# Weight casts, sums and norm scales at other places in the queues of a three-stage fp32 kernel

## The chip, the cores and the metric

The kernel runs on one core of one Trainium2 chip. The metric is the device time of one execution in microseconds, the median of three runs. The engines are called by the short names that the profile uses: PE (TensorE's matmuls; PEld are its weight loads), ACT (ScalarE), DVE (VectorE), POOL (GpSimd) and SP (SyncE, which here issues all DMAs). Each engine works through its own queue in the order in which the program was written.

## The reference

Three stages follow each other, all in fp32: attention with a window, an MLP, and a gated MLP behind an RMS norm. The change touches the end of the second stage and the third.

```
x = attention(q, k, v)                    # 4 x 576 tokens, d = 512, window 128
h = x @ w_in                              # first MLP: 512 -> 2048 -> 512
x = (h * clip(h + 3, 0, 6) / 6) @ w_out
xn = x / sqrt(mean(x * x) + 1e-6) * rms_g # second MLP: 512 -> 2 x 1536 -> 512
g = xn @ w_gate
out = (g * sigmoid(g) * (xn @ w_val)) @ w_out2
```

## The kernel before

**Precision.** Matmuls run on fp32r operands. Each fp32 operand is split into a high part (a cast, made by ACT) and a low part (the rest, a subtraction on DVE), and each product is three matmuls: high x high, high x low, low x high. So every weight and every activation needs one cast and one subtraction before PE can use it.

**First MLP.** The 2304 tokens are taken in six blocks of 384. A block has 16 steps `m`, each with 12 matmuls into the one bank `ps_h` (L465), an activation of two operations (ACT's Relu L693, DVE's `t` L694, which reads `ps_h` and so frees it), the split of the result (ACT `g` L699, DVE `g` L705), and nine matmuls of the second product of the step before (L478).

**Second MLP.** The tokens are taken in three superblocks `s` of 768, and the 1536 hidden columns in 12 chunks `m`. One pair of superblock and chunk is a group `i = 12 s + m`, so there are 36. A group is a 2x2 block product made with seven products instead of eight (`group`): the right operands are seven sums or parts of the inputs (A11, S2, A12, S3, S1, A22, S4), the left ones seven sums or parts of a chunk's weights (B11, T2, B21, T3, T1, T4, B22). Each product is six matmuls of 384 columns (L797) into one of three banks. In a group, ACT copies the first product (`s`, L810), DVE adds it twice (`u`, L813 behind product 1 and L820 behind product 3), and so on; product 2 waits for the copy `s`, product 3 for the first `u`, product 6 for the first `t` (L824), since they add into the banks that these read. The last operation is `t·r` (L834); its cast and subtraction (`g`, L840 and L842) are made within the next group. After the groups m = 0, 2, 4, 6, 8 and 11 comes a round of outputs (`outputs`): six tiles of six matmuls of 512 columns (L853), each added by DVE to `y` (L860), or copied by ACT (L858) in the first round of a superblock. The banks of even and odd groups alternate.

**Weights of the second MLP.** A chunk is read from DRAM as four parts (`load`, tile `tx`, into one of two stages). POOL makes four sums from them (`sums`, L239 to L242), ACT casts them in two halves of 1024 and 768 columns (`high`, L248, tile `th`; the first half needs the third sum), and DVE subtracts in the same halves (`low`, L256, tile `tl`). Both are stored to DRAM as well, and superblocks 1 and 2 fetch them from there (L766) into a ring of three places. Superblock 0 uses what was just made: chunks 0, 1, 2, 11, 10 and 9 are prepared in the last block of the first MLP (EARLY), chunks 3 to 8 in the groups 1 to 6 (the rest of `parts`). Of EARLY the j-th loads at step 2j + 1, sums at 2j + 2, casts at 2j + 3 and 2j + 4, and subtracts at 2j + 4 and 2j + 5.

**Inputs.** The first MLP's result is normed (`Norm`: squares on ACT, the root on POOL, the scale on DVE, L515, then transposes on PE, a copy `yt` on ACT, L520, and a store). A superblock's inputs are loaded as `x2raw` (`Inputs`), scaled by `rms_g` in four parts (L619), added to S1, S2, S4 and S3, and split (L643 on ACT, L647 on DVE). For superblocks 1 and 2 this is done during the superblock before: load after its group 5, scale on DVE after group 7, sums on POOL after group 8, the splits of A11 and S2 after groups 9 and 10, and the other five in group 11 and its outputs, each as soon as PE has used the old one.

Of the kernel before, what the change touches and what calls it, by code (L numbers as in the profile page):

```python
# [10 lines left out]
F32 = mybir.dt.float32  # L11
# [4 lines left out]
AF = mybir.ActivationFunctionType  # L16
ALU = mybir.AluOpType
# [3 lines left out]
P = 128  # L21
B, H, S, D = 4, 8, 576, 64
# [3 lines left out]
KC = DM // P  # L26
F1, F2 = 2048, 1536
M1, M2 = F1 // P, F2 // P
# [41 lines left out]
def fused_kernel(ctx: ExitStack, tc: tile.TileContext, qd, kd, v, w1, w2, rms_g, out):  # L70
# [199 lines left out]
    class Pair:  # L270
# [335 lines left out]
    class Inputs:  # L606
# [2 lines left out]

        def __init__(self, s):  # L610
            self.s, self.n = s, 3 * P
            self.x = xpool.tile([P, KC, 6 * P], F32, tag="xs", name="x2raw")
            sp.dma_start(out=self.x, in_=x2[s])

        def block(self, r, c):
            return self.x[:, 2 * c : 2 * c + 2, r * self.n : (r + 1) * self.n]

        def scale(self, c):
            vec.tensor_scalar(self.x[:, c], self.x[:, c], g_sb[:, c : c + 1], None, ALU.mult)  # L619

        def sum(self, which, on, out):
            setattr(self, which, out)
            x, sub = self.block, on.tensor_sub
            if which == "S1":
                on.tensor_add(out, x(1, 0), x(1, 1))
            elif which == "S2":
                sub(out, self.S1, x(0, 0))
            elif which == "S3":
                sub(out, x(0, 0), x(1, 0))
            else:  # L630
                sub(out, x(0, 1), self.S2)

        def of(self, which):
            return getattr(self, which) if which[0] == "S" else self.block(int(which[1]) - 1, int(which[2]) - 1)
# [13 lines left out]

    ops = {}

    early = [Parts(m, STAGES[j % 2], (RING + SCRATCH)[j]) for j, m in enumerate(EARLY)]
    parts = {m: Parts(m, STAGES[m % 2 == 0], RING[m % 3]) for m in range(3, M2 - 3)}
    outs, slot, late = None, AHEAD, []
    for p, (b, m0, m1) in enumerate(PARTS):
        n = BLOCKS[b][1]
# [13 lines left out]
        for m in range(m0, m1):  # L669
# [58 lines left out]
            if last:  # L728
                if m == 1:
                    fed = Inputs(0)  # L730
                elif m == 2:
# [46 lines left out]
                x.pop(which)()  # L778
        waiting[:] = [x for x in waiting if x]

    def group(i, after):


        s, m = divmod(i, M2)
# [5 lines left out]
        new = parts.get(i + 2)  # L790
        odd = m % 2

        def product(k, ps, start=True):
            x, w, j = ops[s, k], ring[i] if i in ring else parts[i].tiles(), 0
            for c in range(2):
                for a, b in PARTS_OF:
                    pe.matmul(  # L797
                        ps, lhsT=w[a][:, k, c * P : (c + 1) * P], rhs=x[:, b, c],
                        start=(start and j == 0), stop=(j == 5), skip_group_check=True,
                    )  # L800
                    j += 1
            after(k)

        if new and odd:
            new.high(0)
            new.low(0)
        product(0, ps_1)
        if i and i + 3 in parts:
            parts[i + 3].load()
        act.copy(s1, ps_1)  # L810
        settle("high")
        product(1, ps_6)
# [1 line left out]
        settle("low")  # L814
        product(2, ps_1, False)
        act.activation(r[:, 0], ps_1, AF.Silu)
        if new:
            new.high(odd)
        product(3, ps_6, False)
        vec.tensor_add(u[:, 1], s1, ps_6)  # L820
        if new and odd:
            new.low(1)
# [5 lines left out]
        if new and not odd:  # L828
            new.high(1)
        if i + 3 in parts:  # L830
            parts[i + 3].sums()
        product(6, ps_5, False)
        vec.tensor_add(t[:, 0], u[:, 0], ps_5)
        vec.tensor_mul(t, t, r)  # L834
        if i + 3 not in ring and i + 3 not in parts:
            fetch(i + 3)

# [3 lines left out]

        waiting.append({"high": high, "low": lambda: vec.tensor_sub(gs[i][:, 1], t, f32(gs[i][:, 0]))})  # L842

    def outputs(i, spare, after=lambda t: None):


        s, m = divmod(i, M2)
        for t in range(6):
            p, tag = ((ps_out, "o2"), (ps_a, "T"), spare)[t % 3]
# [14 lines left out]
            after(t)  # L864
        fetch_out(i + 4)

    for i in range(M2 * PAIRS2):
        s, m = divmod(i, M2)
        for x in norms:
            x.store()  # L870
            x.scale()
        turn = m == M2 - 1 and s + 1 < PAIRS2
        group(i, (lambda k: fed.high(k) if k > 1 else None) if turn else lambda k: None)
        if i == 0:
            finish1()
            fetch_out(0)
            fetch_out(2)
        if s + 1 < PAIRS2:
            if m == 5:
                fed = Inputs(s + 1)  # L880
            elif m == 7:
                for c in range(KC):
                    fed.scale(c)
            elif m == 8:
                sums = xpool.tile([P, 4, 2, n], F32, tag="xs", name="sums")
                for k in range(4):
                    fed.sum(f"S{(1, 2, 4, 3)[k]}", pool, sums[:, k])
            elif m in (9, 10):
                fed.high(m - 9)
                fed.low(m - 9)  # L890
        spare = banks[(i + 1) % 2][2]
        if m == 0 and s or m in (2, 4, 6, 8):
            x = parts.get(i + 2)
            outputs(i - 2, spare, lambda t: x.low(t // 2) if x and t in (0, 2) else None)
        elif m == M2 - 1:
            outputs(i - 3, spare, lambda t: fed.low(t + 1) if turn and 0 < t else None)
            if turn:
                fed.low(2 + 4)
        if i:
            norms[:] = [x for x in norms if x.back()]  # L900
    settle("high")
    settle("low")
    outputs(M2 * PAIRS2 - 2, banks[0][2])
    p2.close()


# [41 lines left out]
```

## Time and profile before

| | |
|---|---|
| median of 3 runs | 988.22 us (987.93 to 988.41) |
| the profiled execution | 987.71 us; its span, first to last instruction, 985.7 us |
| mean granted clock of PE | 0.996 |
| busy PE / DVE / ACT / POOL | 961.9 / 631.8 / 463.6 / 164.1 us |
| first MLP's last block to its end | until 553.65 us |
| second MLP, superblocks 0 / 1 / 2 from | 553.65 / 693.26 / 834.17 us |

All times in rows are microseconds from the start of the span. The busy times are means over all stages. The engine with the most is PE, and in the timelines an idle stretch of an engine is written in brackets behind the instruction that ended it, with what released it.

### The profile page before, as it was taken

The page shows a single profiled execution, that of the slowest core. Times are in us where ns is not written, and L with a number is a line of the kernel's source. Part 1 is how long each engine was busy: PE and PEld are TensorE (multiplying, and loading weights), DVE is VectorE, ACT ScalarE, POOL GpSimd, SP SyncE. Part 2 cuts the span into 40 slices and gives each one's busy share as a digit, 9 for nine tenths or more (in the row PEclk, how much of TensorE's full clock was granted, in tenths as well). Part 3 has the DMA queues.
Part 4 walks back from the last instruction along what each step waited for, and adds up shares of the span by engine and source line. Part 5 has one row for each costly group of instructions (what it writes and reads, how often), then busy time and mean ns, then how long its engine had stood idle before and what let it go on. Part 6 is the DMA issues. An engine that isn't in the chain of part 4 may idle for free.

```text
span 985.7 us, 14697 instructions
## 1 busy us (share of the span) xinstructions
PE 961.9 (98%) x5448; PEld 845.4 (86%) x5448; DVE 631.8 (64%) x1297; ACT 463.6 (47%) x961; POOL 164.1 (17%) x257
## 2 busy tenths in 40 slices
PE   8999899999999999999998999999999999999998
PEld 5677788888888888888997888989899988999996
DVE  6788863445777766765576657777645678545654
ACT  6799854455666665665454453314132214132120
POOL 4333111121112211111043333130000030000000
PEclk9999999999999999999999999999999999999999
DMA  6446401113665465445356756956655756655521
GB/s 238 150 164 226 180 30 31 49 41 94 190 202 189 151 183 174 154 141 159 128 187 241 286 197 247 335 222 233 232 202 195 275 183 244 241 218 192 202 108 65
DMA packets 67719, 176.85 MB, mean 179 GB/s; under 512 B 5056, under 2 KB 41920, under 8 KB 62912
## 3 DMA queue, kind: packets, MB, share of 16 engines
q1 hardware_dynamic: 67648, 175.92, 50.9%
q8 instruction: 43, 0.70, 0.3%
q14 instruction: 28, 0.23, 0.1%
HBM read 131.86 MB, written 44.04 MB: 178 GB/s over the span
## 4 chain that ended last, share of the span: by engine, by line
PE 83%; DVE 8%; ACT 4%; issue 2%; DMA 1%; POOL 1%; SPq 0%; POOLq 0%; ACTq 0%; DVEq 0%
PE ps_h L465 17%; PE ps_o L478 17%; PE ps_y L853 14%; PE ps_o L797 9%; PE ps_S L797 7%; PE ps_A L797 5%; PE ps_h L797 3%; PE ps_av L402 3%; PE ps_t L389 3%; PE ps_s L349 1%; PE ps_s L340 1%; ACT wx L132 1%; PE warm L553 1%; DVE t L694 1%; DVE y L860 1%
## 5 line engine op out<-in xcount | busy, mean ns | idle before, releaser
L465 PE MATMUL ps_h<-xs,w 128*128 128x384 f32 x1152 | 225.1, 344 | 3.1 <-DVE t L694 3.1
L478 PE MATMUL ps_o<-w,g 128*128 128x512 f32 x864 | 223.7, 401 | 3.0 <-DVE w L143 2.6
L465 PEld LDWEIGHTS ps_h<-xs,w 128*128 128x128 f32 x1152 | 203.8, 191 | 8.8 <-DVE t L694 4.4
L478 PEld LDWEIGHTS ps_o<-w,g 128*128 128x128 f32 x864 | 157.1, 188 | 43.0 <-issue 6.1
L853 PE MATMUL ps_y<-wo,g 128*128 128x512 f32 x648 | 150.7, 390 | 0.5 <-DVE g L842 0.5
L853 PEld LDWEIGHTS ps_y<-wo,g 128*128 128x128 f32 x648 | 121.2, 188 | 25.7 <-DVE g L842 0.9
L694 DVE SCALAR_TENSOR_TENSOR t<-t,ps_h 128x384 f32<-128x384 f32 x96 | 53.2, 554 | 138.6 <-ACT t L693 138.6
L693 ACT ACTIVATE t<-ps_h,three 128x384 f32<-128x384 f32 x96 | 55.7, 580 | 102.2 <-PE ps_h L465 92.8
L377 POOL TENSOR_SCALAR r<-den 128x2 f32<-128x2 f32 x72 | 30.4, 423 | 347.0 <-ACT t L375 345.6
L860 DVE TENSOR_TENSOR y<-y,ps_y 128x512 f32<-128x512 f32 x90 | 61.4, 685 | 37.0 <-PE ps_y L853 36.8
L375 ACT ACTIVATE t<-t,m 128x256 f32<-128x256 f32 (+1 forms) x144 | 69.4, 485 | 7.9 <-DVE m L363 7.9
L699 ACT CAST g<-t 128x384 fp32r<-128x384 f32 x96 | 49.5, 516 | 49.0 <-DVE t L694 45.9
L827 ACT ACTIVATE r<-r 128x384 f32<-128x384 f32 x36 | 18.9, 526 | 113.2 <-DVE r L826 113.2
L797 PE MATMUL ps_o<-S,tw 128*128 128x384 f32 x336 | 65.9, 338 | 0.0
L705 DVE TENSOR_TENSOR g<-t,g 128x384 fp32r<-128x384 f32 x96 | 54.8, 571 | 13.0 <-ACT g L699 11.6
L797 PEld LDWEIGHTS ps_o<-S,tw 128*128 128x128 f32 x336 | 59.4, 188 | 0.4 <-DVE u L813 0.4
L378 POOL TENSOR_TENSOR r<-r,minus 128x2 f32<-128x2 f32 x72 | 56.4, 784 | 6.0
L810 ACT COPY s<-ps_S 128x384 f32<-128x384 f32 x18 | 8.6, 480 | 94.6 <-PE ps_S L797 94.6
L389 PE MATMUL ps_t<-ident,t 128*128 128x128 f32 x272 | 42.2, 275 | 5.2 <-DVE t L383 4.3
L363 DVE CUSTOM_DVE_ANT_0 t<-ps_s,rel 128x256 f32<-128x256 f32 (+2 forms) x128 | 44.7, 394 | 3.3 <-PE ps_s L349 3.3
L394 ACT COPY pt<-ps_t 128x512 f32<-128x512 f32 (+1 forms) x72 | 40.0, 555 | 13.1 <-PE ps_t L389 12.9
L389 PEld LDWEIGHTS ps_t<-ident,t 128*128 128x128 f32 x272 | 33.0, 140 | 14.7 <-ACT t L375 4.3
(135 smaller groups left out, 1472.7 us busy)
## 6 DMA issues: line engine op xcount, KB each, us to landing
tw<-t SPq DMA_DIRECT2D x54, 896.0 KB, 6.3
wraw<-w SPq DMA_DIRECT2D x36, 512.0 KB, 4.3
wo<-w SPq DMA_DIRECT2D x18, 1024.0 KB, 4.8
wraw<-w SPq DMA_DIRECT2D x16, 1024.0 KB, 7.6
t<-th SPq DMA_DIRECT2D x12, 896.0 KB, 4.0
t<-tl SPq DMA_DIRECT2D x12, 896.0 KB, 4.2
b<-wx SPq DMA_DIRECT2D x24, 256.0 KB, 2.5
w<-w SPq DMA_DIRECT2D x12, 512.0 KB, 2.8
```

The costliest lines, as they stand in the source:

```text
L375: act.activation(p, p, AF.Exp, bias=self.m[:, a : a + 1], scale=-1.0, accum_out=self.den[:, a : a + 1])
L378: pool.tensor_tensor(self.r, self.r, minus, ALU.pow)
L389: pe.transpose(self.ps[:, a, c], self.t[:, a, c * P : (c + 1) * P], ident)
L465: pe.matmul(ps[:, : n * P], lhsT=w[:, a, c * P : (c + 1) * P], rhs=xs[c][:, b, : n * P], start=(k == 0), stop=(k == 3 * KC - 1),)
L478: pe.matmul(o, lhsT=g[:, a, i * P : (i + 1) * P], rhs=w[:, b], start=(m == first and a == 0 and b == 0), stop=(m == last and a == 1),)
L693: act.activation(r[:, :nq], ps[:, :nq], AF.Relu, bias=three)
L694: vec.scalar_tensor_tensor(out=r[:, :nq], in0=r[:, :nq], scalar=6.0, in1=ps[:, :nq], op0=ALU.min, op1=ALU.mult)
L699: act.copy(g[:, 0, :nq], r[:, :nq])
L705: vec.tensor_sub(g[:, 1, :nq], r[:, :nq], f32(g[:, 0, :nq]))
L797: pe.matmul(ps, lhsT=w[a][:, k, c * P : (c + 1) * P], rhs=x[:, b, c], start=(start and j == 0), stop=(j == 5), skip_group_check=True,)
L853: pe.matmul(ps, lhsT=gs[i + k][:, a, t // 3, t % 3 * P : (t % 3 + 1) * P], rhs=wo[i + k][:, b], start=(k == 0 and a == 0 and b == 0), stop ...
L860: vec.tensor_add(acc[t], acc[t], ps)
```

## The change

Nothing is computed differently; work moves between places and engines.

- EARLY has four chunks (0, 1, 2, 11) and they stand three steps apart: the j-th loads at step 3j + 1, sums at 3j + 2, casts at 3j + 4 and 3j + 5, subtracts at 3j + 5 and 3j + 6. Chunk 3 is loaded at step 13 and summed at step 15 of the same block.
- `parts` holds chunks 3 to 10, eight and not six. What is done at which place of a group stands in a table `jobs`, filled by a loop over the chunks and by `turn`, and is called by `do(i, place)`: "start", "silu" (behind the first SiLU), "sum" (behind the second `u`), "silu 2", "end", and 0 to 5 for the tiles of the outputs.
- Casts: chunks 3, 4, 6, 8, 10 at "silu" and "silu 2" of the group two before the chunk's own; 5, 7, 9 in the outputs of tiles 4 and 5 of the group three before. Subtractions: even chunks in the outputs of tiles 0 and 2, odd ones at "start" and "sum" of the next group (chunk 3's in group 2).
- The scale and the store of `Norm` move from ahead of a group into it: store at "silu", scale at "sum".
- The inputs of the next superblock are loaded at the start of group 5, scaled by ACT in the outputs of group 6 (DVE after group 7 before), and summed by DVE in the outputs of group 8 (POOL before). The splits of A11 and S2 go to the end of that round: casts behind tiles 4 and 5, subtractions at the start of group 9. The last subtraction (S4), which the code before makes twice, is made once.

```diff
-STAGES, RING, SCRATCH, OUT_W, GS, SUMS = (0, 1), (2, 4, 6), (8, 10, 8), (8, 9), (12, 13, 10, 11), (14, 15)
-EARLY = (0, 1, 2, M2 - 1, M2 - 2, M2 - 3)
+STAGES, RING, SCRATCH, OUT_W, GS, SUMS = (0, 1), (2, 4, 6), 8, (8, 9), (12, 13, 10, 11), (14, 15)
+EARLY = (0, 1, 2, M2 - 1)
...
-    parts = {m: Parts(m, STAGES[m % 2 == 0], RING[m % 3]) for m in range(3, M2 - 3)}
+    parts = {m: Parts(m, STAGES[m % 2 == 0], RING[m % 3]) for m in range(3, M2 - 1)}
...
                 for j, x in enumerate(early):
-                    k = m - 2 * j
+                    k = m - 3 * j
...
-                    if k in (3, 4):
-                        x.high(k - 3)
                     if k in (4, 5):
-                        x.low(k - 4)
-                if m == M1 - 1:
+                        x.high(k - 4)
+                    if k in (5, 6):
+                        x.low(k - 5)
+                if m == M1 - 3:
                     parts[3].load()
+                elif m == M1 - 1:
+                    parts[3].sums()
...
+    for m, x in parts.items():
+        i = m - 2
+        if m > 3:
+            job(i - 1, "start", x.load)
+            job(i - 1, "silu 2", x.sums)
+        if i == 1 or i % 2 == 0:
+            job(i, "silu", x.high, 0)
+            job(i, "silu 2", x.high, 1)
+        else:
+            job(i - 1, 4, x.high, 0)
+            job(i - 1, 5, x.high, 1)
+        if i % 2 == 0:
+            job(i, 0, x.low, 0)
+            job(i, 2, x.low, 1)
+        else:
+            i = max(i, 2)
+            job(i, "start", x.low, 0)
+            job(i, "sum", x.low, 1)
+
+    def turn(s):
+
+        i, x = s * M2, Inputs(s + 1)
+        job(i + 5, "start", x.load)
+        for c in range(KC):
+            job(i + 6, (1, 3)[c // 2], x.scale, c, act)
+        for k, which in enumerate(("S1", "S2", "S4", "S3")):
+            job(i + 8, k, x.later, which, k)
+        for k in range(2):
+            job(i + 8, 4 + k, x.high, k)
+            job(i + 9, "start", x.low, k)
+        for k in range(2, 7):
+            job(i + 11, {2: "silu", 3: "sum", 5: "silu 2"}.get(k, "end"), x.high, k)
+            job(i + 11, k - 1, x.low, k)
...
         for x in norms:
-            x.store()
-            x.scale()
+            job(i, "silu", x.store)
+            job(i, "sum", x.scale)
...
-            elif m == 7:
-                for c in range(KC):
-                    fed.scale(c)
-            elif m == 8:
-                sums = xpool.tile([P, 4, 2, n], F32, tag="xs", name="sums")
-                for k in range(4):
-                    fed.sum(f"S{(1, 2, 4, 3)[k]}", pool, sums[:, k])
```

Three places show what moved. The first is ACT's queue in the last block of the first MLP, from step 8 to step 10 (`t` is the Relu of a step, `th` a chunk's cast, A and S the splits of superblock 0's inputs). Before:

```order
L693 ACTIVATE t<-ps_h,three 128x384
L699 CAST g<-t 128x384
L248 CAST th<-tx 128x768
L693 ACTIVATE t<-ps_h,three 128x384
L699 CAST g<-t 128x384
L248 CAST th<-tx 128x1024
L643 CAST S_5903<-sum 128x768
L693 ACTIVATE t<-ps_h,three 128x384
```

In the change, the same steps:

```order
L703 ACTIVATE t<-ps_h,three 128x384
L709 CAST g<-t 128x384
L248 CAST th<-tx 128x768
L703 ACTIVATE t<-ps_h,three 128x384
L709 CAST g<-t 128x384
L653 CAST S_5885<-sum 128x768
L703 ACTIVATE t<-ps_h,three 128x384
L709 CAST g<-t 128x384
L248 CAST th<-tx 128x1024
```

In step 9 no cast of a chunk stands ahead of the next Relu any more; the next chunk's first cast is in step 10.

The second place is DVE's queue from the end of group 1 to group 2 (`y<-y,ri` is the norm's scale, `tl` a chunk's subtraction, `u` the two sums that PE waits for). Before:

```order
L834 TENSOR_TENSOR t<-t,r 128x768
L515 TENSOR_SCALAR y<-y,ri 128x512
L813 TENSOR_TENSOR u<-s_6294,ps_A 128x384
L842 TENSOR_TENSOR g<-t,g 128x768
L820 TENSOR_TENSOR u<-s_6294,ps_A 128x384
L824 TENSOR_TENSOR t<-u,ps_S_6293 128x384
```

In the change:

```order
L844 TENSOR_TENSOR t<-t,r 128x768
L256 TENSOR_TENSOR tl<-tx,th 128x1024
L828 TENSOR_TENSOR u<-s_6261,ps_A 128x384
L853 TENSOR_TENSOR g<-t,g 128x768
L834 TENSOR_TENSOR u<-s_6261,ps_A 128x384
L256 TENSOR_TENSOR tl<-tx,th 128x768
L515 TENSOR_SCALAR y<-y,ri 128x512
L837 TENSOR_TENSOR t<-u,ps_S_6260 128x384
```

Chunk 3's two subtractions stand ahead of the first `u` and between the second `u` and the first `t`, and the norm's scale has gone behind the second.

The third place is DVE's queue in the outputs of group 8, from the first tile's add to `u` of group 9. Before, these are the rows from group 7's `t·r` to group 9's `u`, with group 8's middle left out:

```order
L834 TENSOR_TENSOR t<-t,r 128x768
L619 TENSOR_SCALAR x2raw<-x2raw,g_sb 128x768 x4
L813 TENSOR_TENSOR u<-s_6919,ps_A 128x384
...
L834 TENSOR_TENSOR t<-t,r 128x768
L860 TENSOR_TENSOR y<-y,ps_y 128x512 x6
L813 TENSOR_TENSOR u<-s_7039,ps_o_7037 128x384
```

In the change, from the second operation of the round on (chunk 10's `tl`, the four `sums`, the splits of A and S):

```order
L256 TENSOR_TENSOR tl<-tx,th 128x1024
L630 TENSOR_TENSOR sums<-x2raw 128x768
L871 TENSOR_TENSOR y<-y,ps_y 128x512
L632 TENSOR_TENSOR sums<-sums,x2raw 128x768
L871 TENSOR_TENSOR y<-y,ps_y 128x512
L256 TENSOR_TENSOR tl<-tx,th 128x768
L636 TENSOR_TENSOR sums<-x2raw,sums 128x768
L871 TENSOR_TENSOR y<-y,ps_y 128x512
L634 TENSOR_TENSOR sums<-x2raw 128x768
L871 TENSOR_TENSOR y<-y,ps_y 128x512 x2
L657 TENSOR_TENSOR A_7018<-x2raw,A_7018 128x768
L657 TENSOR_TENSOR S_7028<-sums,S_7028 128x768
```

The scales of `x2raw` have left the queue ahead of group 8's `u`, and eight operations have come into the round behind it, ahead of group 9's `u`.

## Rows read from the trace of the kernel before

**Rows 1.** The page: busy us, share of the span, instructions of each engine.
```profile
PE 961.9 (98%) x5448; PEld 845.4 (86%) x5448; DVE 631.8 (64%) x1297; ACT 463.6 (47%) x961; POOL 164.1 (17%) x257
```

**Rows 2.** Timeline of PE, last first-MLP block: start, us, operation [idle before <-releaser].
```profile
506.40 2.27 PE L465 MATMUL ps_h<-xs,w 128*128 128x384 f32 x12
...
510.58 2.27 PE L465 MATMUL ps_h<-xs,w 128*128 128x384 f32 x12
...
530.51 3.92 PE L465 MATMUL ps_h<-xs,w 128*128 128x384 f32 x12 [2.50 <-DVE t L694]
...
553.65 0.51 PE L797 MATMUL ps_h<-A,th 128*128 128x384 f32 x2
```

**Rows 3.** Timeline of all engines ahead of 530.51.
```profile
526.45 0.74 POOL L241 TENSOR_TENSOR tx<-tx 128x256 f32<-128x256 f32 x1
...
527.22 1.05 ACT L248 CAST th<-tx 128x1024 fp32r<-128x1024 f32 x1 [3.73 <-POOL tx L241]
...
529.91 0.55 DVE L694 SCALAR_TENSOR_TENSOR t<-t,ps_h 128x384 f32<-128x384 f32 x1
```

**Rows 4.** Windows: length, busy us per engine, PEclk, DMA share, GB/s.
```profile
530.50:534.30 3.80, 3.79 (x13) 3.79 (x14) 3.26 (x3) 1.98 (x3) 3.31 (x4) 0.55 0.47 196
```

**Rows 5.** DMA issues of a chunk's load: count, KB each, median us to landing.
```profile
tx<-b SPq DMA_DIRECT2D x12, 512.0 KB, 5.3
```

**Rows 6.** Timeline of PE in the second MLP.
```profile
563.08 0.51 PE L797 MATMUL ps_S<-A,th 128*128 128x384 f32 x2
...
588.24 0.60 PE L530 MATMUL ps_x<-ident,y 128*128 128x128 f32 x4
588.59 0.60 PE L797 MATMUL ps_S<-A,th 128*128 128x384 f32 x2
...
591.64 0.62 PE L797 MATMUL ps_S<-A,th 128*128 128x384 f32 x2 [0.69 <-ACT s L810]
...
649.28 0.62 PE L797 MATMUL ps_A<-S,th 128*128 128x384 f32 x2 [1.14 <-DVE u L813]
...
662.64 1.21 PE L797 MATMUL ps_S<-A,tw 128*128 128x384 f32 x6
...
709.45 1.23 PE L797 MATMUL ps_S<-A,tw 128*128 128x384 f32 x6
...
712.61 2.27 PE L797 MATMUL ps_o<-S,tw 128*128 128x384 f32 x12
...
732.37 0.87 PE L797 MATMUL ps_S<-A,tw 128*128 128x384 f32 x4
...
778.23 1.05 PE L797 MATMUL ps_S<-A,tw 128*128 128x384 f32 x5
...
850.39 0.86 PE L797 MATMUL ps_S<-A,tw 128*128 128x384 f32 x4
```

**Rows 7.** Timeline of DVE in group 13, undisturbed.
```profile
711.82 0.56 DVE L813 TENSOR_TENSOR u<-s,ps_o 128x384 f32<-128x384 f32 x1 [1.49 <-PE ps_o L797]
...
714.92 0.56 DVE L824 TENSOR_TENSOR t<-u,ps_o 128x384 f32<-128x384 f32 x1 [0.50 <-PE ps_o L797]
...
717.69 0.96 DVE L834 TENSOR_TENSOR t<-t,r 128x768 f32<-128x768 f32 x1
```

**Rows 8.** Timeline of DVE: operations that follow each other without a wait.
```profile
581.78 2.09 DVE L256 TENSOR_TENSOR tl<-tx,th 128x1024 fp32r<-128x1024 f32 x2
...
657.70 1.87 DVE L860 TENSOR_TENSOR y<-y,ps_y 128x512 f32<-128x512 f32 x3
```

**Rows 9.** Timeline of DVE in group 8: scales, and `t·r` beside POOL's sums.
```profile
646.57 2.20 DVE L619 TENSOR_SCALAR x2raw<-x2raw,g_sb 128x768 f32<-128x768 f32 x4
...
655.13 2.65 DVE L834 TENSOR_TENSOR t<-t,r 128x768 f32<-128x768 f32 x1
```

**Rows 10.** Timeline of ACT at the end of group 2's outputs.
```profile
588.43 0.59 ACT L858 COPY y<-ps_y 128x512 f32<-128x512 f32 x1 [0.77 <-PE ps_y L853]
...
591.11 0.48 ACT L810 COPY s<-ps_S 128x384 f32<-128x384 f32 x1
```

More of the change, by code (lines that the diff above doesn't have):

```diff
@@ L631, in sum, with later @@
                 sub(out, x(0, 1), self.S2)
+        def later(self, which, k):
+            if k == 0:
+                self.sums = xpool.tile([P, 4, 2, self.n], F32, tag="xs", name="sums")
+            self.sum(which, vec, self.sums[:, k])
         def of(self, which):
@@ L730, in fused_kernel @@
                     fed = Inputs(0)
+                    fed.load()
                 elif m == 2:
                     for c in range(KC):
-                        fed.scale(c)
+                        fed.scale(c, vec)
                 for j, x in enumerate(early):
-                    k = m - 2 * j
+                    k = m - 3 * j
                     if k == 1:
@@ L779, in settle, with job, do, group @@
         waiting[:] = [x for x in waiting if x]
-    def group(i, after):
+    jobs = {}
+    def job(i, at, f, *args):
+        jobs.setdefault((i, at), []).append((f, args))
+    def do(i, at):
+        for f, args in jobs.pop((i, at), ()):
+            f(*args)
+    def group(i):
         s, m = divmod(i, M2)
@@ L801, in product @@
                     j += 1
[L802 to L806, printed above, removed]
+        do(i, "start")
         product(0, ps_1)
-        if i and i + 3 in parts:
-            parts[i + 3].load()
         act.copy(s1, ps_1)
@@ L816, in group @@
         act.activation(r[:, 0], ps_1, AF.Silu)
-        if new:
-            new.high(odd)
+        do(i, "silu")
         product(3, ps_6, False)
         vec.tensor_add(u[:, 1], s1, ps_6)
-        if new and odd:
-            new.low(1)
+        do(i, "sum")
         product(4, ps_5)
@@ L827, in group @@
         act.activation(r[:, 1], r[:, 1], AF.Silu)
[L828 to L831, printed above, removed]
+        do(i, "silu 2")
         product(6, ps_5, False)
@@ L834, in group @@
         vec.tensor_mul(t, t, r)
+        do(i, "end")
         if i + 3 not in ring and i + 3 not in parts:
@@ L842, in group, with outputs @@
         waiting.append({"high": high, "low": lambda: vec.tensor_sub(gs[i][:, 1], t, f32(gs[i][:, 0]))})
[L844 removed]
+    def outputs(i, by):
         s, m = divmod(i, M2)
         for t in range(6):
[L849 removed]
+            p, tag = ((ps_out, "o2"), (ps_a, "T"), banks[(by + 1) % 2][2])[t % 3]
             ps = p.tile([P, DM], F32, tag=tag, name="ps_y")
@@ L863, in outputs @@
                 sp.dma_start(out=out[row : row + P, :], in_=acc[t])
-            after(t)
+            do(by, t)
         fetch_out(i + 4)
+    for m, x in parts.items():
[12 more added lines that the diff above has]
+            job(i, 2, x.low, 1)
+        else:
+            i = max(i, 2)
[14 more added lines that the diff above has]
+            job(i + 11, k - 1, x.low, k)
     for i in range(M2 * PAIRS2):
         s, m = divmod(i, M2)
+        if m == 0 and s + 1 < PAIRS2:
+            turn(s)
         for x in norms:
-            x.store()
-            x.scale()
-        turn = m == M2 - 1 and s + 1 < PAIRS2
-        group(i, (lambda k: fed.high(k) if k > 1 else None) if turn else lambda k: None)
+            job(i, "silu", x.store)
+            job(i, "sum", x.scale)
+        group(i)
         if i == 0:
@@ L877, in fused_kernel @@
             fetch_out(2)
-        if s + 1 < PAIRS2:
-            if m == 5:
-                fed = Inputs(s + 1)
-            elif m == 7:
-                for c in range(KC):
-                    fed.scale(c)
-            elif m == 8:
-                sums = xpool.tile([P, 4, 2, n], F32, tag="xs", name="sums")
-                for k in range(4):
-                    fed.sum(f"S{(1, 2, 4, 3)[k]}", pool, sums[:, k])
[L888 to L891, printed above, removed]
         if m == 0 and s or m in (2, 4, 6, 8):
-            x = parts.get(i + 2)
-            outputs(i - 2, spare, lambda t: x.low(t // 2) if x and t in (0, 2) else None)
+            outputs(i - 2, i)
         elif m == M2 - 1:
-            outputs(i - 3, spare, lambda t: fed.low(t + 1) if turn and 0 < t else None)
-            if turn:
-                fed.low(2 + 4)
+            outputs(i - 3, i)
         if i:
@@ L902, in fused_kernel @@
     settle("low")
-    outputs(M2 * PAIRS2 - 2, banks[0][2])
+    outputs(M2 * PAIRS2 - 2, M2 * PAIRS2)
     p2.close()
```

13 lines of the change are left out of this document (7 added, 6 removed).

## The prediction

> **What bounds the kernel now.** I read the busy line of the page first: TensorE (PE) is busy for 98% of the span [rows 1]. So other engines cost time only where PE waits for them, and what the change can win is the sum of those waits in the stretch that it touches: the last block of the first MLP, and the second MLP. I then looked for the waits in the timeline of PE, from the starts of its groups, because there even a small loss shows.
>
> In the last block of the first MLP a step is 4.18 us (506.40 to 510.58). Ten steps, 506.40 to 553.65, take 47.25 us where ten clean ones would take 41.8 [rows 2]: 5.4 us are lost, most of it ahead of 530.51, where PE is idle for 2.50 us. The reader is to see the chain behind that: ScalarE (ACT) stood for 3.73 us at a cast `th` until GpSimd (POOL) had made the third weight sum, and since ACT takes its work in order, the Relu of the next step came late, and with it VectorE's (DVE) `t`, which frees the one bank `ps_h` at 529.91 + 0.55 [rows 3]. After that wait the granted clock is 0.55 for 3.8 us, so near its lower level of 1.2 GHz for most of it [rows 4], and the twelve matmuls take 3.92 us where they take 2.27 elsewhere [rows 2]: the 2.5 us wait cost over 4.
>
> In the second MLP the undisturbed measure is 22.92 us for two groups and one round of outputs (709.45 to 732.37), and 1.05 us for one product (three from 709.45 to 712.61) [rows 6]. Against it:
> - groups 1 to 8 of superblock 0 take 99.56 us (563.08 to 662.64) where four such pairs take 91.68 and three sets of transposes some 0.35 each (588.24 to 588.59): 6.8 us lost [rows 6]. Examples: 591.64 (PE waits for ACT's copy `s`) and 649.28 (1.14 us idle for DVE's `u`);
> - groups 9 to 12 take 46.81 (662.64 to 709.45) against 45.84: 1.0 lost;
> - groups 19 to 24, the second turn of superblock, take 72.16 (778.23 to 850.39) against 68.76: 3.4 lost [rows 6].
> In all 16.6 us, the most that the change could give.
>
> **Slack of DVE.** In an undisturbed group the first `u` runs from 711.82 to 712.38, and product 3, which needs its bank, starts at 712.61: 0.23 us of slack. The first `t` ends at 715.48 and product 6 is due at 709.45 + 6 x 1.053 = 715.77: 0.29 us, with 0.50 idle ahead of that `t`. The product `t·r` starts at 717.69 and takes 0.96; the next `u` comes 7.37 after the last, at 719.19 [rows 6, 7]. DVE operations in a row overlap by 0.08 or so (three y adds of 0.68 in 1.87) [rows 8]. So there are three places with room: **at a group's start** with no outputs ahead some 0.85 us (0.62 idle, 0.23 slack), **at "sum"** some 0.8 (0.50 and 0.29), and **over outputs**, from 725.94 (the end of the pair's second `t·r`) to 734.97 (the latest `u`), 9.0 us, of which six y adds take 3.6.
>
> **The change, part by part.**
>
> *Casts of the early chunks three steps apart and four, not six.* Between a chunk's load and its first cast there is one step more (4.18 us), and its stage is reloaded one step after its last read and not in the same step. A transfer takes 5.3 us [rows 5] and three sums 0.74 each with small gaps [rows 3], about 8 us. ACT was 3.73 us late at worst, so one step more covers it. DVE has at most about 4 us in any step (`t`, `g`, one `tl`, one sum or one block's low), no more than before. Gain: the 5.4 us, its slow clock with it. If GpSimd still meets DVE in three steps it is some tenths less; below, the bound is nothing gained.
>
> *Chunk 3's casts behind the SiLU of group 1, norm scales and stores inside the group.* The waits of group 1 go: ACT no longer has a cast of 1024 columns ahead of `s`. In exchange DVE has chunk 3's `tl` at the start of group 2 and at "sum", and the norm's scale at "sum". The two halves of a `tl` take 2.09 [rows 8], by columns 1.2 and 0.9. At group 2's start 1.2 against 0.85: 0.35 late. At "sum" 0.9 and the scale (128x512 with one input; estimated from four of 768 columns in 2.20 [rows 9] at some 0.4) against 0.8: 0.5 late. A pair of matmuls behind a wait takes 0.62 and not 0.51 [rows 6], so 0.1 for each wait: 1.05 in group 2.
>
> *Chunk 5's casts between the y copies, as those of 7, 9 and 10.* ACT's `s` of group 3 starts at 591.11, when product 2 had been due at 588.59 + 2 x 1.053 = 590.70. Ahead of it the 1024 cast (1.05 [rows 3]) goes in front of the last y copy, which has 0.77 idle ahead [rows 10], and delays that by some 0.2; the copy `yt` (size of a y copy, 0.59) goes, and a 768 cast (by columns 0.8) comes. Less overlaps: 591.11 + 0.2 - 1.0 - 0.5 + 0.75 = 590.55, ending 591.0: 0.3 late where it was 0.9. With the 0.1, and "sum" with chunk 5's second half and the third norm scale as in group 2 (0.6): 1.0 in group 3. Groups 5 and 7 have the 768 half alone at "sum", 0.15 each. Groups 4 and 6 get nothing new ahead of `s` or `u`.
>
> So groups 1 to 8 lose 2.3 new, and give back 6.8 less 0.3 that the transposes cause in any case: 4.2 gained. This includes group 8: its four scales of `x2raw` (2.20 ahead of `u` [rows 9]) go to ACT in the round of outputs of group 6, where ACT has no y copies and the transfer has some 15 us.
>
> *The turn's four sums from GpSimd to DVE.* Beside GpSimd's sums `t·r` took 2.65 us, not 0.96 [rows 7, 9]. On DVE they cost four operations of that size, 0.88 each: 3.5 us, and where they lie decides. All are in the outputs of group 8, with chunk 10's two `tl` and two block lows. 3.6 + 2.0 + 6 x 0.88 = 10.9 against 9.0: `u` of group 9 is 1.9 late (2.4 if the operations do not overlap, 0.96 each). I take 1.9 and 0.1. This wait is new, and is the largest left. In the second turn there is no chunk: 8.9 against 9.0, 0.1 late at most (0.4 without overlap).
>
> The Trainium skill (SBUF — State Buffer, section "Who interferes with whom") says that a DVE operation with two SBUF inputs and a GpSimd one that reads SBUF lock each other out for whole instructions. The trace agrees (2.65 for 0.96). By the rule DVE is freed of two lock-outs of 1.7 us in a turn and pays 3.5 for the sums, so this move by itself is worth nothing; the sum here books nothing to it either, and takes the gain from the place that the sums and scales leave.
>
> *Lows and highs of the turn.* A and S of groups 9 and 10 move into group 8's round; the last low, which before is made twice at the end of group 11's and 23's, is made once. The 1.0 of groups 9 to 12 and its like in the second turn go.
>
> **Sum.** First MLP -5.4; groups 1 to 8 -4.2; groups 9 to 12 -1.0 + 2.0; second turn -3.4 + 0.1. Net -11.9 us. The profiled execution took 987.7 us (span 985.7), 0.5 below the median of 988.2; from that median: 976.3 us.
>
> **Rivals.**
> 1. *GpSimd in DVE's way.* The chunk sums (seven in the second MLP's groups 1 to 7) start when their load lands and could meet a `tl` at "sum" or `u`'s predecessors; each hit costs at most the 1.7 us above, more likely 0.5. Six hits: +3, 979.3 us. For it: the contention is seen [rows 9]. Against: most loads land off those places.
> 2. *The clock.* The 1.9 us wait in group 9 may bring the lower clock as the 2.50 us wait did [rows 2, 4], and the 1.14 us wait at 649.28 did not: some 1.7 us more, 978.0.
> 3. *The change does not reach the first MLP's waits.* If the casts are still late there, say by contention with DVE, half or all of the 5.4 stays: 979 to 981.7. Against it: the wait is one for POOL, and gets a step.
> 4. *The other side.* Chunk 5's load now waits for the second `tl` of chunk 3 at "sum" of group 2, so some 6 us into the group; its cast is due some 15 us into it, and transfer and three sums take about 8. About 1 us of room. From there each us that the transfer is late goes through ACT's queue to `s` of group 3, one for one. It decides only if the load takes 13 us more than the 5.3 of the median: 989 us or above.
>
> **How the numbers follow.** Forecast 0.60 (its own range 974.5 to 978.5), rival 1 0.15, rival 2 0.10, rival 3 0.09, rival 4 0.02; 0.04 for gains given back in ways that I do not see, within 0.2% (some 2 us, about what a measurement of this kernel can tell from no change). The ends: all new waits halved gives 974; rivals 1 and 3 together 982. I give 974 to 982.5. Faster 0.94, same 0.04, slower 0.02.
>
> **What would show it.** Right: the ten steps from step 6 of the last block on in 42 us and no stretch of clock near 0.5; PE's waits in group 1 gone; one wait of some 1.9 us for `u` in group 9, with DVE busy without a gap from group 8's first y add to it; groups 19 to 24 in some 69 us; waits of some 0.4 to 0.6 in groups 2 and 3. Wrong: PE idle for a cast in the last block, ACT waiting for POOL at chunk 5, or a slow clock in group 9. The least certain is the size of the wait in group 9, and whether the half us in groups 2 and 3 is there.

## The result

The changed kernel takes 975.5 us (median of four, 975.14 to 976.61) beside 988.08 us of the kernel before (four, 987.38 to 988.41): ratio 0.9876, interval 0.9858 to 0.9893. So it is 12.6 us faster; 976.3 had been predicted. A later measurement of the same two kernels gave 976.97 and 989.49 us, ratio 0.9871 (0.9851 to 0.9892).

The page of the changed kernel begins with busy us, share of the span and instructions of each engine, and answers to [rows 1]:

```profile
PE 958.7 (98%) x5448; PEld 845.5 (87%) x5448; DVE 626.2 (64%) x1295; ACT 468.8 (48%) x969; POOL 151.8 (16%) x249
```

That line shows nearly nothing: PE does the same matmuls and stands at 98% as before. POOL has lost 12 us and ACT won 5. What the change did is in the starts of the groups. The timeline of PE, to be laid beside [rows 2] and [rows 6] (start, us, operation, and in brackets the idle time ahead). The bracket counts from the end that the profile gives the matmul before, so it comes out a little smaller than the delay of a start:

```profile
508.18 2.27 PE L465 MATMUL ps_h<-xs,w 128*128 128x384 f32 x12
...
550.21 0.51 PE L817 MATMUL ps_h<-A,th 128*128 128x384 f32 x2
...
559.64 0.51 PE L817 MATMUL ps_S<-A,th 128*128 128x384 f32 x2
...
574.18 0.62 PE L817 MATMUL ps_S<-S,th 128*128 128x384 f32 x2 [0.26 <-DVE t L837]
...
586.14 0.62 PE L817 MATMUL ps_S<-A,th 128*128 128x384 f32 x2
...
590.89 0.61 PE L817 MATMUL ps_o<-S,th 128*128 128x384 f32 x2 [0.27 <-DVE t L837]
...
654.67 0.51 PE L817 MATMUL ps_S<-A,th 128*128 128x384 f32 x2
...
659.62 0.62 PE L817 MATMUL ps_o<-S,th 128*128 128x384 f32 x2 [1.64 <-DVE u L828]
...
702.48 0.69 PE L817 MATMUL ps_S<-A,tw 128*128 128x384 f32 x3
...
771.26 1.05 PE L817 MATMUL ps_S<-A,tw 128*128 128x384 f32 x5
...
840.10 1.21 PE L817 MATMUL ps_S<-A,tw 128*128 128x384 f32 x6
```

Each stretch is the difference of two starts:

| stretch | before | after | difference | predicted |
|---|---|---|---|---|
| ten steps from step 6 of the last block | 47.25 | 42.03 | -5.22 | -5.4 |
| groups 1 to 8 | 99.56 | 95.03 | -4.53 | -4.2 |
| groups 9 to 12 | 46.81 | 47.81 | +1.00 | -1.0 + 2.0 |
| groups 13 to 18 | 68.78 | 68.78 | 0 | 0 |
| groups 19 to 24 | 72.16 | 68.84 | -3.32 | -3.4 + 0.1 |

With 0.6 behind that (0.27 in group 28, 0.31 from the start of group 35 to the end) it is 12.65 us. The profiled spans differ by only 10.9 (985.7 and 974.8): the changed kernel's execution came to step 6 of the last block 1.8 us later, a loss at the launch (last section).

The largest wait that is left is the one of group 9. The timeline of DVE ahead of it, from the first tile of group 8's outputs:

```profile
648.22 0.68 DVE L871 TENSOR_TENSOR y<-y,ps_y 128x512 f32<-128x512 f32 x1
648.82 1.22 DVE L256 TENSOR_TENSOR tl<-tx,th 128x1024 fp32r<-128x1024 f32 x1
649.95 0.95 DVE L630 TENSOR_TENSOR sums<-x2raw 128x768 f32<-128x768 f32 x1
...
657.29 0.95 DVE L657 TENSOR_TENSOR A<-x2raw,A 128x768 fp32r<-128x768 f32 x1
658.15 0.95 DVE L657 TENSOR_TENSOR S<-sums,S 128x768 fp32r<-128x768 f32 x1
659.02 0.55 DVE L828 TENSOR_TENSOR u<-s,ps_o 128x384 f32<-128x384 f32 x1
```

No row has an idle time in brackets: DVE works from 648.22 to `u` without a gap, 10.8 us in a place with room for 9.0. PE's product 3 was due at 657.83 and starts at 659.62. The window around the wait (length, busy us of PE, PEld, DVE, ACT, POOL, then PEclk, DMA share, GB/s) has the full clock, unlike [rows 4]:

```profile
657.60:661.60 4.00, 2.36 (x14) 2.05 (x13) 3.39 (x5) 0.49 (x1) 0.00 (x0) 1.00 0.72 291
```

### The profile page after: what moved, and what is told of

It is laid out like the page before. It is cut to its first block, busy times and chain, and to the rows that moved or that the text cites. A ratio compares the mean times of both kernels' runs of the same rounds, so it can differ in the third digit from the quotient of the medians.

```text
span 974.8 us, 14681 instructions
## 1 busy us (share of the span) xinstructions
PE 958.7 (98%) x5448; PEld 845.5 (87%) x5448; DVE 626.2 (64%) x1295; ACT 468.8 (48%) x969; POOL 151.8 (16%) x249
## 4 chain that ended last, share of the span: by engine, by line
PE 89%; DVE 5%; ACT 3%; issue 1%; DMA 1%; POOL 0%; ACTq 0%; POOLq 0%; DVEq 0%; SPq 0%
PE ps_o L478 19%; PE ps_h L465 19%; PE ps_y L864 14%; PE ps_o L817 9%; PE ps_S L817 8%; PE ps_A L817 6%; PE ps_h L817 4%; PE ps_av L402 3%; PE ps_t L389 3%; PE ps_s L349 2%; PE ps_s L340 1%; PE warm L553 1%; ACT wx L132 1%; PE ps_x L530 1%; DMA wraw<-w 1%
## 5 line engine op out<-in xcount | busy, mean ns | idle before, releaser
L465 PE MATMUL ps_h<-xs,w 128*128 128x384 f32 x1152 | 222.8, 341 | 0.1
L465 PEld LDWEIGHTS ps_h<-xs,w 128*128 128x128 f32 x1152 | 201.6, 189 | 4.9 <-PE warm L553 0.5
L478 PEld LDWEIGHTS ps_o<-w,g 128*128 128x128 f32 x864 | 157.0, 188 | 43.1 <-issue 5.8
L817 PE MATMUL ps_o<-S,tw 128*128 128x384 f32 x312 | 61.1, 338 | 0.0
L817 PEld LDWEIGHTS ps_o<-S,tw 128*128 128x128 f32 x312 | 55.2, 188 | 0.1
```

The costliest lines, as they stand in the source:

```text
L465: pe.matmul(ps[:, : n * P], lhsT=w[:, a, c * P : (c + 1) * P], rhs=xs[c][:, b, : n * P], start=(k == 0), stop=(k == 3 * KC - 1),)
L478: pe.matmul(o, lhsT=g[:, a, i * P : (i + 1) * P], rhs=w[:, b], start=(m == first and a == 0 and b == 0), stop=(m == last and a == 1),)
L817: pe.matmul(ps, lhsT=w[a][:, k, c * P : (c + 1) * P], rhs=x[:, b, c], start=(start and j == 0), stop=(j == 5), skip_group_check=True,)
```

## The experiments

Medians of different experiments stand on different chips and at different launches, so the small differences below are read from the starts of the groups, counted from group 0 (or from step 6 for the last block). They agree to 0.07 us between the two profiles of the changed kernel, and to 0.2 in the last block.

**1. Early chunks two steps apart again, still four.**

```diff
-                    k = m - 3 * j
+                    k = m - 2 * j
...
-                    if k in (4, 5):
-                        x.high(k - 4)
-                    if k in (5, 6):
-                        x.low(k - 5)
+                    if k in (3, 4):
+                        x.high(k - 3)
+                    if k in (4, 5):
+                        x.low(k - 4)
```

> The change with one part undone: the four early chunks stand two steps apart again and not three (casts at the second and third step behind the load, as before); chunks 3 to 10 stay where the change has them. Theory (the distance is what removed the waits): the casts of the third early chunk (step 7 of the last block) and of the fourth (step 9) are late again, PE idle some 0.5 us and some 2.5 us, the second wait with the granted clock near 0.55 behind it for some 3.8 us; ten steps from step 6 on take 46 to 47 us where the change takes 42.0, the whole some 980.4 us (+4.9). Rival (fewer chunks in the block is what helped, less DMA and less work): ten steps within 0.5 us of 42.0, the whole within 0.5 of 975.5. Everything behind the block, from group 1 on, unchanged in both.

Measured: ten steps 43.1 us, 0.24 more in group 1, all else as in the change; 978.06 us. Neither theory. The waits return at the two places named, but the second is 0.46 us and not 2.5, and the clock stays up. Either two chunks fewer made the difference, or the 2.50 us of [rows 2] is not what the old order always does. The two kernels had a difference that I had passed over: SP issued the load of step 7 (PE is then in step 8) in 1.44 us before, and in 0.62 here.

**2. The kernel before, once more, and (3.) before without the second S4 subtraction.** The first is unchanged. The second:

```diff
-            if turn:
-                fed.low(2 + 4)
```

> The kernel before, unchanged, for a second profile of it. In its first profile the load at step 8 of the last block was issued in 1.44 us and the fourth early chunk was summed so late that PE stood 2.5 us; with four chunks at the same two steps it was issued in 0.62 us, POOL's first sum began 1.1 us earlier in the step and was not held up by DVE, and PE stood about half a us. Theory A (the 2.5 us wait belongs to the order of before): ten steps from step 6 take 46 to 47.5 us again, a stretch of half clock with them. Theory B (the load is on the edge, and a late issue tips it: by luck of an execution): ten steps take 43.5 to 45 us, no stretch of half clock there, the fourth chunk's first sum ahead of DVE's subtraction of that step.

> The kernel before with one part of the change alone: the last subtraction of the turn (S4), which it makes twice at the end of groups 11 and 23, is made once. Theory: the second one stands ahead of u of groups 12 and 24 and is worth some 0.65 us in each: -1.3 us by the starts of the groups from 11 on. Rival: DVE has room there, nothing. The ten steps of the last block give a further look at before's waits: 46 to 47.5 us if they belong to its order, 43.5 to 45 if they hang on when a load is issued.

Measured: 987.31 and 985.98 us. Ten steps took 47.09 us in the first and 44.12 in the second, whose last block is the same code. Both theories of the first have their execution, then. Timeline of SP, POOL and PE in the first:

```profile
519.15 1.67 SPq L235 DMA_DIRECT2D tx<-b  x1
...
526.09 1.29 POOL L239 TENSOR_TENSOR tx<-tx 128x256 f32<-128x256 f32 x1 [6.79 <-DMA tx<-b]
...
532.34 3.42 PE L465 MATMUL ps_h<-xs,w 128*128 128x384 f32 x12 [2.50 <-DVE t L694]
```

and in the second:

```profile
518.29 0.57 SPq L235 DMA_DIRECT2D tx<-b  x1
...
523.58 0.74 POOL L239 TENSOR_TENSOR tx<-tx 128x256 f32<-128x256 f32 x1 [5.13 <-DVE sum L631]
...
529.47 0.81 PE L465 MATMUL ps_h<-xs,w 128*128 128x384 f32 x3 [0.48 <-DVE t L694]
```

Where the load is issued in 0.57 us, POOL starts 5.29 us after the issue began and gets through in 0.74; where it takes 1.67, POOL starts 6.94 us after, and needs 1.29 beside DVE's subtraction. PE then stands 2.50 and not 0.48 us, and the lower clock comes on top (0.63 granted in the 3.8 us behind). So of the 5.2 us that the change gained in the last block, 2.1 (44.12 less 42.03) are lost in the old order even with the short issue, and some 3.1 more, with another 0.2 in group 1, where that load is issued slowly.

The second subtraction of S4 cost what was expected: 0.63 us in group 12 and 0.67 in group 24. A further 0.27 went in group 28; its cause stays open.

**4. The load at that step made later** (run 1, with two loads of 2 KB ahead of it).

```diff
+    g_no = [const.tile([P, KC], F32, name=f"g_no{k}") for k in range(2)]
...
                     if k == 1:
+                        if j == 3:
+                            for t in g_no:
+                                sp.dma_start(out=t, in_=rms_g)
                         x.load()
```

> The run with four early chunks two steps apart, and two loads of 2 KB (128 x 4 numbers each, used by nothing) in SP's queue ahead of the load of step 7, the one that was issued in 1.44 and 1.67 us in the two profiles of before with a 2.5 us wait, and in 0.57 and 0.62 us in the two profiles without. Theory (the load stands on an edge: landed some 0.8 us later, POOL's first sum meets DVE's subtraction, ACT's cast, the Relu behind it and PE are late one behind the other): load issued some 0.8 us later, POOL's first sum takes 1.3 us and not 0.74, PE idle some 2.3 to 2.5 us in step 9, half clock behind it, ten steps 46 to 47 us where they took 43.4. Rival (the wait has another cause, and the long issue only went with it): each 0.1 us of issue costs 0.1 us of wait and no more, ten steps 43.4 to 44.4, no half clock.

Measured: ten steps 46.78 us, 982.51 us in all. Timeline of SP, POOL and PE:

```profile
521.98 0.57 SPq L236 DMA_DIRECT2D tx<-b  x1
...
526.95 1.39 POOL L240 TENSOR_TENSOR tx<-tx 128x256 f32<-128x256 f32 x1 [6.70 <-DVE g L716]
...
533.29 1.03 PE L466 MATMUL ps_h<-xs,w 128*128 128x384 f32 x4 [2.48 <-DVE t L705]
```

The two small loads took 1.83 us of SP, more than meant. By the traces' landing times the load is there 0.3 us after step 9's first matmul, as in the two profiles with the long issue (0.4), and not 1.2 us ahead of it, as in experiments 1 and 3. That makes the whole picture of those two profiles: POOL's sum of 1.39 us, PE idle for 2.48, and a granted clock of 0.60 in the 3.7 us behind it. A load that lands late is a sufficient cause, and two chunks fewer do not prevent it. Why SP takes 0.6 us in one execution and 1.4 to 1.7 in another stays open; the long issue of this load was seen in two of the three profiles with six early chunks and in none of the ten with four.

**5. The changed kernel, once more.**

> The changed kernel, unchanged, for a second profile and for times beside those of the runs of this call. If the cover in the last block holds whatever the issue of the loads does: ten steps 42.0 to 42.2 us again, the starts of all groups within 0.1 us of the first profile counted from group 0; only the launch (first step at 38.4 to 40.7 us) may differ. If the first profile was a lucky one: ten steps 43 us or more.

Measured: ten steps 42.21 us, all groups within 0.07 us. In its order no such wait appeared in any of the eight profiles that have casts three steps apart (42.0 to 42.3 us). But in all eight the load of the fourth early chunk was issued in 0.57 us, so none of them shows what a late one would do. The timeline of POOL and ACT in the change has the third sum of that chunk and its first cast:

```profile
534.57 1.60 POOL L241 TENSOR_TENSOR tx<-tx 128x256 f32<-128x256 f32 x1
...
541.58 1.04 ACT L248 CAST th<-tx 128x1024 fp32r<-128x1024 f32 x1
```

The sum ends 5.4 us ahead of the cast. A third sum that is 2.0 us later, as that of experiment 2 is beside that of experiment 3, would still be in time; this is an estimate.

**6. The scales of `x2raw` back on DVE.**

```diff
-            job(i + 6, (1, 3)[c // 2], x.scale, c, act)
+            job(i + 7, "end", x.scale, c, vec)
```

> The change with one part undone: the four scales of x2raw are on DVE again, at the end of groups 7 and 19, and not on ACT in the outputs of groups 6 and 18. Theory (the place in DVE's queue is the cost): four scales take 2.2 us against some 0.85 of room ahead of u of groups 8 and 20, so u is some 1.3 us late in each, with 0.1 of slower matmuls behind it: +2.8 us, 978.3. Rival (GpSimd's sums beside DVE were what made those groups late, and they are gone in both): within 0.5 us of the change.

Measured: 983.0 us; +4.87 us in group 8 and +1.40 in group 20. Group 20 is the theory to the tenth. Group 8 is far more, and the timeline of DVE, POOL and PE shows why:

```profile
639.13 1.05 POOL L239 TENSOR_TENSOR tx<-tx 128x256 f32<-128x256 f32 x1 [9.90 <-DMA tx<-b]
639.50 4.11 DVE L624 TENSOR_SCALAR x2raw<-x2raw,g_sb 128x768 f32<-128x768 f32 x4
...
644.12 0.76 PE L817 MATMUL ps_A<-S,th 128*128 128x384 f32 x2 [3.02 <-DVE u L828]
...
783.89 2.20 DVE L624 TENSOR_SCALAR x2raw<-x2raw,g_sb 128x768 f32<-128x768 f32 x4
...
786.61 0.62 PE L817 MATMUL ps_A<-S,tw 128*128 128x384 f32 x2 [1.15 <-DVE u L828]
```

The same four operations take 2.20 us alone and 4.11 beside chunk 10's sums on POOL. The wait of 3.02 us that follows brings the lower clock, in the window behind it:

```profile
644.20:648.00 3.80, 3.80 (x13) 3.80 (x14) 1.29 (x2) 0.00 (x0) 0.00 (x0) 0.55 0.02 4
```

So 1.3 us of place, 1.9 of POOL, and the rest, some 1.7, of the clock. The theory holds in both groups. The rival, no more than 0.5 us in all, fails; only its mechanism shows, in group 8, by chunk 10's sums and not by those of the turn. The two moves of the change support each other, since eight chunks put POOL's sums where the scales used to be.

**7. The four sums back on POOL.**

```diff
-            self.sum(which, vec, self.sums[:, k])
+            self.sum(which, pool, self.sums[:, k])
```

> The change with one part undone: the four sums of the next superblock's inputs are made by GpSimd again, written at the same places of group 8's and 20's outputs; everything else as in the change. Theory A (each engine on its own): DVE is rid of 3.5 us, the wait of u in group 9 (1.8 + 0.1) goes and nothing comes: -1.9 us, 973.6. Theory B (DVE operations with two inputs stand still beside GpSimd's): DVE operations in the round take 2.0 us or more in place of 0.9, four sums of some 2 us on GpSimd give three or four such hits of 1.7 us each, and the casts of A and S on ACT come later too: group 9's wait stays between 1.5 and 4 us, the whole between 975 and 978.

Measured: 976.05 us; by the starts +0.75 in group 8 and its outputs, -1.81 in group 9, +0.27 in group 19, in all -0.78 us. Theory A counts only the middle one. Theory B saw the cost but not where it falls: `u` of group 9 is in time, since the DVE operations held up lie early in the round. Timeline of POOL, DVE and PE:

```profile
648.02 2.44 POOL L636 TENSOR_TENSOR sums<-x2raw,sums 128x768 f32<-128x768 f32 x1
...
649.27 2.27 DVE L256 TENSOR_TENSOR tl<-tx,th 128x1024 fp32r<-128x1024 f32 x1
...
652.19 1.20 PE L864 MATMUL ps_y<-wo,g 128*128 128x512 f32 x4 [0.44 <-DVE y L871]
```

A `tl` takes 2.27 and not 1.22, a y add behind it comes late, and PE waits within the outputs. The move of the sums is thus no gain by itself (the prediction booked nothing to it); it costs 0.8 us as the rest of the change stands.

**8. A11's and S2's subtractions out of `u`'s way.**

```diff
-            job(i + 9, "start", x.low, k)
+            job(i + 9 + k, "silu 2", x.low, k)
```

> The change with one step moved: the subtractions of A11 and S2 for the next superblock leave the place ahead of u of groups 9 and 21 and go to the place behind the second SiLU, one in group 9 (21) and one in group 10 (22). Theory (group 9's wait is DVE's queue length alone): two operations of 0.88 us fewer ahead of u, the wait of 1.8 us falls to 0.1 or nothing and the 0.1 behind it goes, and in groups 9 and 10 the moved operations lie in idle time of DVE: -1.75 us, 973.8. Rival (u is late for another reason, the last y adds behind PE's outputs or ACT's s): the wait stays above 1 us, the whole within 0.6 us of the change.

Measured: -1.74 us in group 9, -1.78 in all; 974.57 us. The wait was the length of DVE's queue; 0.06 us and the 0.1 behind it are left.

**9. All subtractions out of the way, and (10.) two more moves.** First the edit of 8 and

```diff
-            i = max(i, 2)
-            job(i, "start", x.low, 0)
-            job(i, "sum", x.low, 1)
+            job(*((i, "silu 2") if i == 1 else (i, "start")), x.low, 0)
+            job(*((2, "start") if i == 1 else (i, "silu 2")), x.low, 1)
```

then, on top of it,

```diff
-            job(*((2, "start") if i == 1 else (i, "silu 2")), x.low, 1)
+            job(*((2, "sum") if i == 1 else (i, "silu 2")), x.low, 1)
...
-            job(i, "sum", x.scale)
+            job(i, "silu 2", x.scale)
```

> The change with all subtractions moved that stand ahead of a waited operation of DVE: those of A11 and S2 as in the run before (behind the second SiLU of groups 9 and 10), chunk 3's to the second SiLU of group 1 and the start of group 2, the second half of chunks 5, 7 and 9 from the second u to the second SiLU. Theory: of the waits in groups 2, 3, 5 and 7, 1.7 us in all, some 1.6 go, on top of the 1.75 of the turn: 3.3 us less than the change by the starts of the groups, about 972.2 us. Rival (DVE's casts moved to the second SiLU hold up the second t or t*r instead, or the load that waits for them): half of it or less on top of the turn, 973 or above.

> The run with all subtractions moved, and two more moves: chunk 3's second subtraction from the start of group 2 to the second u of group 2, and the norm's scale from the second u to the second SiLU in all groups. Theory: the first u of group 2 (0.57 + 0.10 late there) has nothing new ahead of it, the first t of group 2 has 0.95 us of subtraction ahead of it in place of 0.48 of scale against some 0.8 of room, so 0.1 to 0.3 late with its 0.1: 0.3 to 0.5 us less than that run by group 3's start, 3.2 to 3.4 us less than the change by the last group. Rival (the subtraction of the first half at the second SiLU of group 1 had made t*r late, and u of group 2 with it): u stays late by 0.3 or more, no gain.

Measured: the first is 2.85 us shorter than the change by the starts (974.68 us), 0.5 less than the theory. The missing half us is the rival's: chunk 3's subtraction at the second SiLU makes `t·r` of group 1 late, and with the half still ahead of it PE waits 0.56 us for `u` of group 2, more than the 0.29 in the change. The second repairs that: 3.10 us shorter than the change, 972.53 us beside 989.49 of the kernel before in the same measurement, ratio 0.9833 (0.9812 to 0.9853). It is the fastest version found. Its wait in group 9, on PE's timeline (0.17 us by the starts), is too short for a bracket:

```profile
655.65 0.62 PE L817 MATMUL ps_o<-S,th 128*128 128x384 f32 x2
```

**11. Chunk 5's load later.**

```diff
+            last_at = "silu 2" if i == 1 else "sum"
             i = max(i, 2)
             job(i, "start", x.low, 0)
-            job(i, "sum", x.low, 1)
+            job(i, last_at, x.low, 1)
```

> The change with chunk 3's second subtraction two places later in group 2 (behind the second SiLU), so that the load of chunk 5, which takes its stage, is issued some 2.2 us later. Theory (chunk 5's sums then end some 0.5 us after ACT asks for them, and ACT's queue hands that on to s of group 3): the wait at the second u of group 2 goes (-0.5), s of group 3 is 0.5 later: within 0.3 us of the change in group 4's start. Rival (the late sums hide in ACT's idle time): -0.5 us by group 4's start, and nothing new in group 3.

Measured: -0.53 us in group 2, +0.30 in group 3, 975.91 us. Timeline of POOL, ACT and PE:

```profile
579.06 0.74 POOL L239 TENSOR_TENSOR tx<-tx 128x256 f32<-128x256 f32 x1 [9.82 <-DMA tx<-b]
...
581.45 1.05 ACT L248 CAST th<-tx 128x1024 fp32r<-128x1024 f32 x1 [0.19 <-POOL tx L241]
...
584.24 0.47 ACT L825 COPY s<-ps_S 128x384 f32<-128x384 f32 x1
...
584.76 0.62 PE L817 MATMUL ps_S<-A,th 128*128 128x384 f32 x2 [0.21 <-ACT s L825]
```

ACT waits for POOL's third sum, and `s` of group 3 is late by it. The direction is the theory's, the size (0.30 for 0.5) under two thirds of it. The load starts POOL 2.4 us later counted from group 0, but the sums now take 0.74 us each where two of them take 1.10 and 1.34 in the change, beside DVE. Rival 4's chain exists, then. In the change it has room, as ACT's and POOL's timelines show, the third sum ending at 581.12 and the cast that needs it starting at 582.83 behind a y copy:

```profile
577.78 1.10 POOL L239 TENSOR_TENSOR tx<-tx 128x256 f32<-128x256 f32 x1 [7.42 <-DMA tx<-b]
...
580.38 0.74 POOL L241 TENSOR_TENSOR tx<-tx 128x256 f32<-128x256 f32 x1
...
582.83 1.05 ACT L248 CAST th<-tx 128x1024 fp32r<-128x1024 f32 x1
```

## Why the prediction was right, and where it was right by luck

- **First MLP, -5.4.** Measured -5.2 between the two profiles first taken, and the chain (POOL's sum, ACT's cast, Relu, `t`, PE) is as told. The 0.2 that it falls short are the "some tenths" for GpSimd beside DVE: in step 9 of the change a `tl` takes 1.75 us and a sum 1.49 beside POOL's sums, and `t` comes late. But the step "5.4 us are lost" took one execution for the order. Experiments 2 to 4 split it: 2.1 us with the short issue too, 3.1 more where the load at that step lands late. Beside an execution with the short issue the gain is some 9.3 us by the starts (12.65 less 3.1 and the 0.2 of group 1). One step more between load and cast was worth 1.1 us in the ten steps and 0.24 in group 1 (experiment 1), two chunks fewer, with what else differs in the block, 1.0 (44.12 less 43.11).
- **The luck in it.** The profiled executions of the old order have a mean granted clock of 0.996 with the long issue and 0.998 with the short. Of 51 further executions of the kernel before, 27 have 0.997 or less and took 987.3 to 991.5 us; 24 have 0.998 or more, and all but two of these took 984.2 to 988.1. The times that the forecast was worked out from and measured against (987.4 to 988.4) fit the first. Beside an execution of the second kind the forecast gain of 11.9 us would have been some 2.6 too large. All nine executions of the changed kernel have 0.998 or more, so the clock's drop did not come in it; whether its order covers a late load or only does not meet one is not shown.
- **Groups 1 to 8, -4.2.** Measured -4.5. The new waits in group 2 were 0.29 and 0.42 with 0.1 each (predicted 0.35 and 0.5), at "sum" of group 3 it was 0.43 and 0.10 (0.6 in all predicted), in groups 5 and 7 0.14 each (0.15). The term most mis-sized is `s` of group 3: 0.3 + 0.1 predicted, 0.08 + 0.10 measured (the pair at 586.14). Its sum had the last y copy delayed by 0.2 by the cast ahead; the copy started at 583.77, the cast's end having cost it 0.07.
- **Groups 9 to 12, +1.0.** The wait of 1.9 + 0.1 was 1.79 + 0.11. Sizes of single DVE operations and their overlap, taken from an undisturbed group, were enough.
- **Second turn, -3.3.** Measured -3.32.
- **Rivals.** GpSimd in DVE's way cost the 0.2 us of the last block and no PE time in the second MLP of the changed kernel, though it was near: experiment 6 shows what one hit at the wrong place costs, 1.9 us and then the clock. The clock did not drop behind 1.64 us of idle time (PEclk 1.00). The waits of the first MLP did not stay. Rival 4's chain was confirmed by experiment 11; in the change it had 1.7 us of room (581.12 to 582.83), where about 1 had been predicted.

## What to carry to other kernels

With one engine at 98%, lay the starts of equal pieces of work beside those of an undisturbed piece: the differences add up to the time, term by term, where the busy shares say nothing. Before a wait of one profile is booked as a gain, look whether it is there in a second one: here a load that landed 1.6 us later in some executions cost PE 3.1, and the median of a few runs does not tell how many of them had it. Where an in-order engine feeds the bound, ask of each operation what stands behind it; moving two operations of 0.9 us by half a group was worth their full length.

## What the runs showed of the hardware

- **Launch.** In eight of 13 profiles the first step of the first MLP starts between 38.4 and 39.1 us, in five between 40.3 and 40.7, with nothing changed ahead of it. They are told apart by PE's warm-up matmuls: from 7.4 us at the latest a pair takes 0.70 us in the eight, and in the five still 1.22 at 8.06. PE's timeline of the kernel before, one of the eight, and of the change, one of the five:

```profile
6.72 0.70 PE L553 MATMUL warm<-rel 128*128 128x256 f32 x2
```

```profile
8.06 1.22 PE L553 MATMUL warm<-rel 128*128 128x256 f32 x2
```

  The windows of 5.0 to 8.5 us show a PEclk of 1.00 in both, with 18 and 12 matmuls in them. But the traces' entries of the granted clock begin at 5.1 to 6.5 us in the eight and only at 11.1 to 11.8 in the five, and the pairs get fast at about that moment (the one at 5.75 us in experiment 6 takes 0.87 with the first entry at 6.14). So the five's 1.00 ahead of it has no entry behind it, and their pace there fits the 1.2 GHz level. An effect of 2 us must be read behind this.
- **DVE beside POOL.** Not only operations with two inputs are held up: four one-input scales took 4.11 us beside POOL's sums and 2.20 alone, and POOL's own sums 0.92 to 1.05 and not 0.74. The y adds, which read one input from PSUM, took 0.68 beside POOL as elsewhere (experiment 7). The Trainium skill (SBUF — State Buffer, section "Who interferes with whom") says that a `tensor_scalar` can run in a mode that takes both port pairs, the one shared with GpSimd too; the trace agrees for the scales (4.11 us for 2.20).
- **Clock.** Idle stretches of PE of 2.30 (in attention, ahead of 124.06 in the kernel before), 2.48, 2.50 (twice) and 3.02 us in these runs were followed by 3.7 to 3.8 us with a granted clock of 0.55 to 0.63, so mostly the 1.2 GHz level; 1.14, 1.15 and 1.64 us were not followed by any drop.
- **Issue of a load.** One and the same load of 512 KB was issued in 0.57 to 0.62 us in some executions and in 1.44 to 1.67 in others. What decides it stays open.
